# One core: attention and two MLPs, with the first 320 queries' probabilities kept in fp32 and turned by TensorE

## The chip, the cores and the metric

One core of a Trainium2 chip runs the program. The metric is device microseconds (us) of one execution; lower is better. The time of a kernel is the median of its runs. Engines: PE is TensorE's matmul side, PEld its weight load, DVE VectorE, ACT ScalarE, POOL GpSimd, SP the sync engine that issues DMAs.

## The reference

q, k and v are fp32, the MLPs' weights 64-bit floats. For most products the kernel splits a value into a high and a low fp16 half. Batch 4, 8 heads, 576 positions, head size 64; model width 512, inner width 2048.

```python
q_rot, k_rot = rotate(q), rotate(k)
scores = q_rot @ k_rot^T / sqrt(D)
scores = scores - max(scores, axis=-1)
attn = exp(scores)
attn = attn / (sum(attn, axis=-1) + 1e-9)
x = (attn @ v), heads side by side            # 2304 x 512
h = x @ moe_w_in;   x = (h * sigmoid(1.702 h)) @ moe_w_out
h = x @ moe2_w_in;  x = where(h > 0, h, exp(h) - 1) @ moe2_w_out
```

## The kernel before

**Tiling.** The 2304 queries are cut into nine blocks: batch 0 into three (128, 192 and 256 queries, the numbers 0, 1 and 2), every other batch into two (320 and 256). The 8 heads are worked on in pairs, hp 0 to 3. A unit (`s_units`) is one chunk of 128 queries of one head pair, or the last 64 queries of both heads laid on the two halves of the partitions (the tail). For each unit PE makes the fp32 scores (L689), DVE takes the negative row maximum (L694), ACT the exponentials with their sums (L698, tile E), DVE the reciprocal (L705, L709). Then the probabilities are scaled and split: the fp16 high half by ACT or DVE (`hi`, L714 or L716), the fp16 remainder by DVE (`lo`, L720), both in one tile Ehl. A transposing DMA on SP (L729, for a tail L726) writes them turned, keys on the partitions, into the tile et.

**Product with V.** `av_unit` multiplies et with V, which has been scaled and split into fp16 halves as well (`v_prep`, L652 and L655, with three small DMAs L659 to L661 that shift copies by half a tile): 14 products per head, the two heads on the two column halves of the array (L757). ACT and DVE write the result as two fp16 halves x (L760, L764).

**MLPs.** `first_mlp` multiplies x of the four head pairs with W1i (L808, 12 matmuls per unit of 128 inner columns), ACT and DVE form the activation (L811, L814, L823, L826, into ghl), and L845 multiplies with W1o; the results go to DRAM (y_d). The second MLP reads them back (L1040 to L1167).

**Weights.** `Weight` loads 64-bit pieces of 128 x 512 (L418; W1i's into ghl, which is empty then, W1o's into its own end), makes fp32 of them (ACT L425 and L432, DVE L439 and L444), takes a bound of their norms by PE (L462: sums against ones, gathered in one PSUM bank per weight that is held from the first sum to the last), brings the maximum over partitions (L346, L350, L353), and then scales and splits in place (ACT L499 or DVE L501, and DVE L505).

**What sets the order.** The program is a plan: `op` notes an operation with the engines that can run it and a cost on each, the operations that it follows, a key and the buffers that it needs. `Plan.run` goes through an own clock, gives every free engine the ready operation of the smallest key whose buffers are free, and emits the instructions in that order. TUNE holds numbers that are added to keys or costs, BUFS how many buffers there are: two score tiles of two banks each, one bank for products with V, and three banks "m" for everything else on PE (turns of q and k, L808, L845, sums). So engines work through fixed lists of instructions, and another number in TUNE is another list on every engine.

**The beginning.** `prep` loads k and q of one head pair on SP (four DMAs, L563 and L564), DVE applies the rotation with a table `tab` (L568, L572, L576), PE turns the result (L581, with the identity `eye`), ACT copies it out of PSUM (L586). `start` loads `eye` and `tab` on SP (L544, L545).

## Time and profile before

| | |
|---|---|
| runs | 1043.17, 1038.73, 1040.77 us; median 1040.77 |
| profiled execution | 1040.95 us, span in the trace 1039.2 us |
| PE busy | 959.6 us (92%), 7754 instructions |
| DVE busy | 864.1 us (83%), 1695 instructions |
| ACT busy | 603.8 us (58%), 1161 instructions |
| mean granted clock of PE | 0.954 of 2.4 GHz |
| DMA | 109.44 MB in 224062 packets, 372 issues |

The profile's times begin with the span. A group of rows gives for each line, engine and shape the count, the busy time, the mean of one, and the idle time ahead of it with its releaser. A busy sum is a share of the whole span; what a stage is worth is read from the stretch in which it lies.

### The profile page before, as it was taken

Reading aid. Unit: us, or ns where it says so; the run is one execution under the profiler, and the core shown is the slowest. Engines: PE = TensorE matmul, PEld = TensorE weight load, DVE = VectorE, ACT = ScalarE, POOL = GpSimd, SP = SyncE. Lnnn points to the kernel's source line nnn. Section 1 sums busy time; section 2 is a strip of 40 time slices with the busy share of each in tenths; the row PEclk is TensorE's granted clock in tenths of the full one; section 3 lists DMA queues with packets and bytes.
Section 4 is the critical chain, followed back from the end, with each engine's and each line's share of the span. In section 5 each row is a group of like instructions: output and inputs, shape, how many; then the busy total and the mean of one; then the engine's idle time right before and its main releaser. Section 6 shows DMA issues by size and latency. Waiting matters only on the chain. (4 is left out here: it accounts for less than half of the span.)

```text
span 1039.2 us, 19888 instructions
## 1 busy us (share of the span) xinstructions
PE 959.6 (92%) x7754; PEld 682.4 (66%) x7754; DVE 864.1 (83%) x1695; ACT 603.8 (58%) x1161; POOL 0.4 (0%) x6
## 2 busy tenths in 40 slices
PE   2447899999999999999999999999989999999997
PEld 2225588877766677766688778644436845855886
DVE  6999999887999689888765969899999579579474
ACT  4788797675687577666453739575355145145142
POOL 0000000000000000000000000000000000000000
PEclk8555899999999999999999999999999999999999
DMA  8899757896678856755635433610000100100100
GB/s 261 299 232 203 136 82 133 153 184 114 135 132 183 126 104 123 134 92 109 110 71 164 161 108 108 216 43 1 29 13 21 51 11 18 50 16 5 42 16 21
DMA packets 224062, 109.44 MB, mean 105 GB/s; under 512 B 187872, under 2 KB 213088, under 8 KB 223968
## 3 DMA queue, kind: packets, MB, share of 16 engines
q1 hardware_dynamic: 223968, 108.17, 46.7%
q8 instruction: 61, 1.00, 0.4%
q14 instruction: 33, 0.27, 0.1%
HBM read 53.61 MB, written 9.44 MB: 61 GB/s over the span
## 5 line engine op out<-in xcount | busy, mean ns | idle before, releaser
L808 PE MATMUL m<-x,wi 128*128 128x256 f16 (+3 forms) x1728 | 199.9, 275 | 2.1 <-DVE wi L505 1.7
L845 PE MATMUL m<-ghl,wo 128*128 128x256 f16 (+3 forms) x1728 | 198.2, 273 | 0.2 <-DVE wo L505 0.2
L1040 PE MATMUL m<-yhl,w2i 128*128 128x512 f16 (+1 forms) x960 | 190.2, 360 | 4.7 <-DVE e L1051 4.5
L808 PEld LDWEIGHTS <-wi 128*128 128x128 f16 x1728 | 157.6, 99 | 45.7 <-issue 14.7
L845 PEld LDWEIGHTS <-wo 128*128 128x128 f16 x1728 | 155.7, 98 | 41.7 <-issue 12.5
L1040 PEld LDWEIGHTS <-w2i 128*128 128x128 f16 x960 | 94.4, 98 | 98.5 <-issue 7.8
L698 ACT ACTIVATE E<-s,st 128x576 f32<-128x576 f32 x144 | 106.0, 737 | 67.8 <-DVE st L694 60.8
L720 DVE SCALAR_TENSOR_TENSOR Ehl<-E,st,Ehl 128x576 f16<-128x576 f32 x144 | 114.8, 810 | 9.9 <-ACT Ehl L714 9.5
L694 DVE TENSOR_REDUCE st<-s 128x1 f32<-128x576 f32 x144 | 106.4, 749 | 7.9 <-PE s L689 7.8
L689 PE MATMUL s<-qkT 64*128 64x288 f32 (+1 forms) x640 | 108.2, 459 | 4.1 <-ACT E L698 4.0
L714 ACT ACTIVATE Ehl<-E,st 128x576 f16<-128x576 f32 x105 | 79.9, 772 | 31.3 <-DMA et<-Ehl 10.1
L1043 ACT ACTIVATE e<-m,y_c 128x512 f32<-128x512 f32 (+1 forms) x80 | 50.7, 637 | 73.2 <-issue 48.7
L689 PEld LDWEIGHTS s<-qkT 64*128 64x128 f32 (+1 forms) x640 | 56.4, 189 | 33.1 <-issue 10.6
L1116 PEld LDWEIGHTS <-g 128*128 128x128 f16 x714 | 69.5, 98 | 8.7 <-issue 0.7
L811 ACT ACTIVATE t<-m,hsc 128x320 f32<-128x320 f32 (+3 forms) x96 | 55.3, 576 | 18.6 <-PE m L808 17.4
L1136 DVE SCALAR_TENSOR_TENSOR x<-z,eo,x 128x256 f32<-128x256 f32 x49 | 23.4, 482 | 48.9 <-PE z L1116 48.6
L823 ACT ACTIVATE ghl<-t 128x320 f16<-128x320 f32 (+3 forms) x96 | 49.7, 520 | 19.5 <-DVE t L814 19.2
L757 PE MATMUL av<-et,v 128*64 128x256 f16 (+3 forms) x720 | 52.8, 291 | 6.6 <-DMA et<-Ehl 5.9
L814 DVE SCALAR_TENSOR_TENSOR t<-t,m 128x320 f32<-128x320 f32 (+3 forms) x96 | 52.5, 547 | 7.6 <-ACT t L811 6.9
L826 DVE SCALAR_TENSOR_TENSOR ghl<-t,ghl 128x320 f16<-128x320 f32 (+3 forms) x96 | 52.6, 550 | 6.1 <-ACT ghl L823 5.9
L1116 PE MATMUL z<-wo,g 128*128 128x256 f16 x504 | 56.3, 273 | 0.0
L1051 DVE SCALAR_TENSOR_TENSOR e<-m,y_c,e 128x512 f32<-128x512 f32 (+1 forms) x80 | 55.0, 690 | 0.4
(160 smaller groups left out, 1233.1 us busy)
## 6 DMA issues: line engine op xcount, KB each, us to landing
R<-in_moe_w_out_dram SPq DMA_DIRECT2D x18, 512.0 KB, 3.7
ghl<-in_moe_w_in_dram SPq DMA_DIRECT2D x16, 512.0 KB, 6.1
R<-in_moe_w_in_dram SPq DMA_DIRECT2D x16, 512.0 KB, 4.2
wo<-in_moe_w_out_dram SPq DMA_DIRECT2D x14, 512.0 KB, 5.8
R<-in_k_dram SPq DMA_DIRECT2D x16, 256.0 KB, 3.0
R<-in_q_dram SPq DMA_DIRECT2D x16, 256.0 KB, 3.4
V<-in_v_dram SPq DMA_DIRECT2D x4, 1024.0 KB, 6.9
R<-y_d SPq DMA_DIRECT2D x8, 512.0 KB, 4.0
```

The costliest lines, as they stand in the source:

```text
L689: nc.tensor.matmul(o, X[r, t:t + (TAIL if h is None else P)], X[r, NS * w:NS * w + NS], start=True, stop=True)
L694: nc.vector.tensor_reduce(out=st["t"][:, a:a + 1], in_=take(hS[a])[:, :, 0:NS], axis=AX.XY, op=ALU.max, negate=True)
L698: nc.scalar.activation(out=take(hE[a]).rearrange("p (c f) -> p c f", c=2), in_=take(hS[a])[:, :, 0:NS], func=AF.Exp, bias=t[:, a:a + 1], s ...
L714: nc.scalar.activation(out=X16[:, 0:S], in_=take(hE[a]), func=AF.Copy, scale=r)
L720: nc.vector.scalar_tensor_tensor(out=X16[:, S:2 * S], in0=E, scalar=r, in1=X16[:, 0:S], op0=ALU.mult, op1=ALU.subtract)
L757: nc.tensor.matmul(ps[64 * a:64 * a + 64, 0:N], W[:, a, j, :] if w == 2 else V[:, w, a, j, :], T[:, a, blk, 0:N], start=i == 0, stop=i == ...
L808: nc.tensor.matmul(ps, W1i.lhs(kk, u, wl), x[:, xl, 0:N], start=kk == 0 and i == 0, stop=kk == KD - 1 and i == 2)
L811: nc.scalar.activation(out=flat(ht), in_=flat(hM), func=AF.Tanh, scale=hsc[b][:, 1:2])
L845: nc.tensor.matmul(ps[:, 0:N], W1o.lhs(f, d, wl), (gh, gl)[xl][:, f, g0:g0 + N], start=f == 0 and i == 0, stop=f == KF - 1 and i == 2)
L1040: nc.tensor.matmul(ps[:, 0:n], W2i.lhs(kk, u, wl), Y[:, xl, kk, 0:n], start=kk == 0 and i == 0, stop=kk == KD - 1 and i == 2)
L1051: nc.vector.scalar_tensor_tensor(out=t[:, 0:n], in0=take(hM)[:, 0:n], scalar=st["c"][:, 0:1], in1=t[:, 0:n], op0=ALU.mult, op1=ALU.max)
L1116: nc.tensor.matmul(ps, AT[A](p, gi, P * tt), BT[B](p, wl), start=p == 0 and i == 0, stop=p == 7 and i == 2)
```

## The change

Blocks 0 and 1 (the first 320 queries of batch 0, `WHOLE`) take another way from the exponentials to x. The probabilities stay fp32: one operation scales E in place (`norm`, by ACT or DVE), L761 or L763 of the changed kernel; there is no remainder and no Ehl. PE turns E against the identity, four blocks of 128 keys for each head and chunk (`turn`, L768), and the last 64 keys of both heads by a plain product (`turn_tail`, L774); ACT or DVE copies them from a bank "m" to et, read as fp32 (`put`, `put_tail`, L778 or L780). The product takes raw fp32 V: ten matmuls, the two heads on the column halves (`mm32`, L827 and L829), and V's scale enters when x is split. No transposing DMA is issued for these blocks. V of batch 0 is still split, since block 2 needs it. The loads of `tab` and `eye`, in the other sequence, and W1i's first two pieces are issued by ACT's queue. TUNE has other numbers everywhere and two new ones, so every engine's list is new; from the second half of PE's list to its end the lists are the same instructions in the same order.

```diff
 TUNE = dict(
...
+    w2i2=-436.9305624813725, w2o2=-980.4720244049131, pt=438.78214921243733, pv=136.99546015091275,
...
+    WHOLE = (0, 1)
...
-                    nc.sync.dma_start(out=flat(c).bitcast(I32), in_=s)
+                    ENG[e].dma_start(out=flat(c).bitcast(I32), in_=s)
...
-                ld = op(*dma_in(P * 4096), load, after, kc, need=[(stage(c), h)])
+                cost = dma_in(P * 4096)
+                if tag == "w1i" and i < 2:
+                    cost = {"act": 500}, cost[1]
+                ld = op(*cost, load, after, -1e6 if tag == "w1i" and i < 2 else kc, need=[(stage(c), h)])
...
     def start(e):
-        nc.sync.dma_start(out=eye, in_=tab_d[:, 18:20, :].rearrange("p a d -> p (a d)"))
-        nc.sync.dma_start(out=tab, in_=tab_d[:, 0:18, :])
+        ENG[e].dma_start(out=tab, in_=tab_d[:, 0:18, :])
+        ENG[e].dma_start(out=eye, in_=tab_d[:, 18:20, :].rearrange("p a d -> p (a d)"))
...
-    begin = op({"dma": 480}, 1600.0, start, key=TUNE["tab"])
+    begin = op({"act": 1000}, 3200.0, start, key=-2e6)
...
-            nc.vector.tensor_scalar(out=t, in0=t, scalar1=1e-9, scalar2=DOWN, op0=ALU.add, op1=ALU.mult)
+            nc.vector.tensor_scalar(out=t, in0=t, scalar1=1e-9, scalar2=1.0 if n in WHOLE else DOWN, op0=ALU.add, op1=ALU.mult)
...
+        if n in WHOLE:
+            hP = [("tp", i, x) for x in range(2 if h is None else 3)]
...
+            def norm(e, a):
+                r, E = st["t"][:, 4 + a:5 + a], take(hE[a])
+                if e == "act":
+                    nc.scalar.activation(out=E, in_=E, func=AF.Copy, scale=r)
+                else:
+                    nc.vector.tensor_scalar(out=E, in0=E, scalar1=r, scalar2=None, op0=ALU.mult)
+
+            def turn(e, a):
+                ps = take(hP[a])
+                for c in range(4):
+                    nc.tensor.transpose(ps[:, P * c:P * c + P], take(hE[a])[:, P * c:P * c + P], eye)
+
+            def turn_tail(e):
+                ps = take(hP[-1])
+                for a in range(2):
+                    x = a if h is not None else 0
+                    nc.tensor.matmul(ps[64 * a:64 * a + 64, 0:m], take(hE[x])[:, 512:S], eye if h is not None else eye[:, 64 * a:64 * a + 64], start=True, stop=True)
...
+            od = []
+            for a in heads:
+                od.append(op({"act": c_act(S, ptr=1), "dve": c_dve(S, 2, ptr=1)}, lambda e, a=a: norm(e, a), [o5], key + a, use=[hE[a]], port=True))
+                ot = op({"pe": 4 * 107 + 100.0}, lambda e, a=a: turn(e, a), od[-1:], key + a - TUNE["pt"], need=[("m", hP[a])], use=[hE[a]])
+                trs.append(op({"act": c_act(512, True) + (50 if h is None else 0), "dve": c_dve(512) + (60 if h is None else 0)}, lambda e, a=a: put(e, a), [ot], key + a - TUNE["pv"], use=[hP[a], hT]))
+            ot = op({"pe": 2 * 280.0}, turn_tail, od, key + 1 - TUNE["pt"], need=[("m", hP[-1])], use=hE)
+            trs.append(op({"act": c_act(m, True), "dve": c_dve(m)}, put_tail, [ot], key + 1 - TUNE["pv"], use=[hP[-1], hT]))
+            return
...
+        def mm32(e):
+            T, ps = take(hT).rearrange("p a s f -> p (a s f)").bitcast(F32), take(hA)
+            for c in range(5):
+                for a in range(2):
+                    r = slice(64 * a, 64 * a + 64)
+                    V = take(("vs", b))[:, 2 * hp + a, c, :]
+                    if c < 4:
+                        k = (4 * a + c) * N
+                        nc.tensor.matmul(ps[r, 0:N], V, T[:, k:k + N], start=c == 0, stop=False)
+                    else:
+                        nc.tensor.matmul(ps[r, 0:N], V[r], T[r, 8 * N:9 * N], start=False, stop=True)
...
-            nc.scalar.activation(out=take(hx)[:, 0, 0:N], in_=take(hA)[:, 0:N], func=AF.Copy, scale=DOWN)
+            nc.scalar.activation(out=take(hx)[:, 0, 0:N], in_=take(hA)[:, 0:N], func=AF.Copy, scale=vsc[b]["s"] if w else DOWN)
```

How the lists move is shown at three places. In the rows a name's number tells one tile or buffer from another.

The first is the beginning of the queues that issue DMAs. SP before (R is the tile of k and q of a head pair, ghl takes W1i's raw pieces):

```order
L563 DMA R_85<-in_k_dram 128x2x256
L564 DMA R_85<-in_k_dram 64x2x64
L563 DMA R_85<-in_q_dram 128x2x256
L564 DMA R_85<-in_q_dram 64x2x64
L544 DMA eye<-in_rope_dram 128x128
L545 DMA tab<-in_rope_dram 128x1152
L418 DMA ghl<-in_moe_w_in_dram 128x1024 x2
```

and in the changed kernel SP, and after it ACT:

```order
L567 DMA R_87<-in_k_dram 128x2x256
L568 DMA R_87<-in_k_dram 64x2x64
L567 DMA R_87<-in_q_dram 128x2x256
L568 DMA R_87<-in_q_dram 64x2x64
L419 DMA ghl<-in_moe_w_in_dram 128x1024 x2
```

```order
L548 DMA tab<-in_rope_dram 128x1152
L549 DMA eye<-in_rope_dram 128x128
L419 DMA ghl<-in_moe_w_in_dram 128x1024 x2
L426 ACT_TABLE_LOAD
L426 ACTIVATE wi<-ghl 128x512 x2
```

The table has gone from the sixth place of SP's list to the first of ACT's, and SP's own first four are the same.

The second is DVE at block 0's last head pair. Before (E_661 and E_665 are its two heads' exponentials, Ehl_706 and Ehl_716 their halves):

```order
L705 TENSOR_SCALAR st<-st 128x2
L709 RECIPROCAL st<-st 128x2
L716 TENSOR_SCALAR Ehl_706<-E_661,st 128x576
L716 TENSOR_SCALAR Ehl_716<-E_665,st 128x576
L764 SCALAR_TENSOR_TENSOR x_714<-av_669,x_714 128x128
L505 SCALAR_TENSOR_TENSOR wi<-wi,w1i_s 128x512
L694 TENSOR_REDUCE st<-s_708 128x1
L720 SCALAR_TENSOR_TENSOR Ehl_706<-E_661,st,Ehl_706 128x576
L694 TENSOR_REDUCE st<-s_710 128x1
L505 SCALAR_TENSOR_TENSOR wi<-wi,w1i_s 128x512
L720 SCALAR_TENSOR_TENSOR Ehl_716<-E_665,st,Ehl_716 128x576
```

and in the changed kernel (E_608 and E_646 are that pair; ACT scales the other head's):

```order
L713 TENSOR_SCALAR st<-st 128x2
L717 RECIPROCAL st<-st 128x2
L763 TENSOR_SCALAR E_608<-E_608,st 128x576
L509 SCALAR_TENSOR_TENSOR wi<-wi,w1i_s 128x512
L428 TENSOR_SCALAR wo<-wo 128x512
L838 SCALAR_TENSOR_TENSOR x_673<-av_649,v_s,x_673 128x128
L505 TENSOR_SCALAR wi<-wi,w1i_s 128x512
L440 SCALAR_TENSOR_TENSOR wo<-wo 128x512
L702 TENSOR_REDUCE st<-s_667 128x1
```

The two remainders L720 are gone, and DVE goes from one scaling to W1i's remainders (L509) and W1o's conversion (L428, L440) and on to the next maxima.

The third is PE after a product of block 1 (av_966 before is its first head pair, s_1008 the scores of its third). Before:

```order
L757 LDWEIGHTS vsh_380
L757 MATMUL av_966<-et_803,vsh_380 64x192
L346 MATMUL m_1005<-eye,v_a 1x128
L689 MATMUL s_1008<-qkT_238 128x288
L689 MATMUL s_1010<-qkT_238 128x288
```

and in the changed kernel the work between a unit of L885 and the product of block 1's first head pair (E_702, E_726 and E_730 its exponentials, m the banks, et_790 the turned ones):

```order
L885 MATMUL m_753<-x_738,wi 128x128
L768 MATMUL m_794<-eye,E_726 128x128 x4
L774 MATMUL m_803<-eye,E_702 64x128
L774 MATMUL m_803<-eye,E_726 64x128
L768 MATMUL m_808<-eye,E_730 128x128 x4
L774 MATMUL m_817<-eye,E_730 64x64 x2
L697 MATMUL s_824<-qkT_202 64x288 x4
L827 MATMUL av_833<-et_790,V_112 64x192 x8
L829 MATMUL av_833<-et_790,V_112 64x192 x2
```

Turns of four blocks and small products against the identity (two of the pair's three turns are in these rows) stand in PE's list where before transposing DMAs stood in SP's, and each has a bank "m" of its own.

## Rows read from the trace of the kernel before

**Rows 1.** Busy time in stretches: us, then PE, PEld, DVE, ACT, POOL busy, PEclk, DMA share, GB/s
```profile
8.30:62.50 54.20, 20.16 (x140) 14.65 (x140) 50.65 (x79) 40.13 (x77) 0.00 (x0) 0.61 0.90 291
62.50:95.50 33.00, 19.62 (x178) 12.68 (x178) 30.63 (x66) 24.29 (x48) 0.00 (x0) 0.50 0.97 216
95.50:131.50 36.00, 29.97 (x320) 21.96 (x320) 34.14 (x80) 28.45 (x64) 0.00 (x0) 0.81 0.77 143
0.00:95.50 95.50, 39.79 (x318) 27.34 (x318) 81.27 (x144) 65.71 (x124) 0.44 (x6) 0.61 0.90 256
137.82:1039.20 901.38, 883.55 (x7049) 627.61 (x7046) 743.09 (x1456) 504.79 (x965) 0.00 (x0) 1.00 0.41 88
```

**Rows 2.** Timeline of PE from the first L808 to 174 us: start, us, what
```profile
97.62 3.40 PE L808 MATMUL m<-x,wi 128*128 128x128 f16 x48
...
105.08 1.02 PE L757 MATMUL av<-et,v 128*64 128x192 f16 x20
105.93 0.50 PE L757 MATMUL av<-et,vsh 128*64 128x192 f16 x8
106.36 0.38 PE L346 MATMUL m<-eye,v_a 128*1 128x128 f32 x2
...
107.84 1.51 PE L808 MATMUL m<-x,wi 128*128 128x128 f16 x24
...
131.47 0.23 PE L808 MATMUL m<-x,wi 128*128 128x128 f16 x1 [1.68 <-DVE wi L505]
...
137.82 0.83 PE L845 MATMUL m<-ghl,wo 128*128 128x128 f16 x12
...
140.57 1.24 PE L689 MATMUL s<-qkT 64*128 64x288 f32 x8
...
171.25 0.55 PE L581 MATMUL m<-eye,T 128*128 128x128 f32 x3
...
172.90 0.88 PE L581 MATMUL m<-eye,T 128*128 128x128 f32 x6
```

**Rows 3.** Waits of PE, 138 to 620 us: us in total, times, longest
```profile
PE av L757 <- DMA et<-Ehl: 1.8, 4, 0.7
...
PE m L581 <- ACT qkT L586: 0.8, 1, 0.8
```

**Rows 4.** Waits of DVE before the mark, and of PE from 62 us to it
```profile
DVE T L568 <- DMA tab<-in_rope_dram: 8.4, 1, 8.4
...
PE av L757 <- DMA et<-Ehl: 4.0, 5, 2.0
```

**Rows 5.** The SP queue at the start, and issues: KB each, median us to landing
```profile
0.73 0.46 SPq L563 DMA_DIRECT2D R<-in_k_dram  x1
...
2.68 0.62 SPq L564 DMA_DIRECT2D R<-in_q_dram  x1
...
3.98 0.43 SPq L545 DMA_DIRECT2D tab<-in_rope_dram  x1
...
tab<-in_rope_dram SPq DMA_DIRECT2D x1, 576.0 KB, 4.3
R<-in_k_dram SPq DMA_DIRECT2D x16, 32.0 KB, 3.1
```

**Rows 6.** Groups by shape: count, busy us, mean ns, idle before
```profile
L720 DVE SCALAR_TENSOR_TENSOR Ehl<-E,st,Ehl 128x576 f16<-128x576 f32 x144 | 114.8, 810 | 9.9 <-ACT Ehl L714 9.5
...
L586 ACT ACTIVATE qkT<-m 128x384 f32<-128x384 f32 x48 | 22.1, 489 | 10.0 <-PE m L581 9.4
...
L505 DVE SCALAR_TENSOR_TENSOR wi<-wi,w1i_s 128x512 f16<-128x512 f32 x16 | 11.8, 741 | 0.0
```

**Rows 7.** Timeline of PE at the lower clock: one turn group and one score group
```profile
38.24 0.87 PE L581 MATMUL m<-eye,T 128*128 128x128 f32 x3 [0.64 <-DVE T L576]
...
77.57 2.29 PE L689 MATMUL s<-qkT 64*128 64x288 f32 x8
```

More of the change, by code (lines that the diff above doesn't have):

```diff
@@ L580, in turn @@
             for s in range(3):
-                nc.tensor.transpose(ps[:, P * s:P * s + P], take(hT)[:, 3 * g + s].rearrange("p h d -> p (h d)"), eye)
+                t = take(hT)[:, 3 * g + s].rearrange("p h d -> p (h d)")
+                nc.tensor.transpose(ps[:, P * s:P * s + P], t, eye)
         def put(e, g):
@@ L610 @@
     v_scaled = {}
+    v_loaded = {}
     def v_view(b, hp):
@@ L623, in ld_ @@
                 nc.sync.dma_start(out=t[64 * a:64 * a + 64, :, 4, :], in_=v[b, :, 512:S, :].rearrange("h p d -> p h d"))
-        ld = op(*dma_in(1311e3, 3), ld_, [], ka, need=[("V", h)])
+        ld = v_loaded[b] = op(*dma_in(1311e3, 3), ld_, [], ka, need=[("V", h)])
         for hp in range(NP):
@@ L644, in v_prep @@
         for hp in range(NP):
+            if all(n in WHOLE for n in range(NB) if blocks[n][0] == b):
+                break
             ks = last_u[fb[b], hp] - TUNE["vs"]
@@ L740, in s_units, with whole, out_, put @@
         cost = dma_tr(2 * S) if h is not None else ({"dma": 2600}, 1700.0)
+        if n in WHOLE:
+            hP = [("tp", i, x) for x in range(2 if h is None else 3)]
+            m = TAIL if h is None else P
+            o = N - TAIL if h is None else chunks.index(j) * P
+            def whole():
+                T = take(hT).rearrange("p a s f -> p (a s f)").bitcast(F32)
+                return T[:, 0:8 * N].rearrange("p (a c f) -> p a c f", a=2, c=4), T[:, 8 * N:9 * N]
+            def norm(e, a):
[13 more added lines that the diff above has]
+                    nc.tensor.matmul(ps[64 * a:64 * a + 64, 0:m], take(hE[x])[:, 512:S], eye if h is not None else eye[:, 64 * a:64 * a + 64], start=True, stop=True)
+            def out_(e, dst, src):
+                if e == "act":
+                    nc.scalar.activation(out=dst, in_=src, func=AF.Copy)
+                else:
+                    nc.vector.tensor_copy(dst, src)
+            def put(e, a):
+                T, ps = whole()[0], take(hP[a])
+                if h is None:
+                    for a in range(2):
+                        out_(e, T[:, a, :, o:o + m], ps.rearrange("p (c a f) -> p a c f", c=4, a=2)[:, a])
+                else:
+                    out_(e, T[:, a, :, o:o + m], ps.rearrange("p (c f) -> p c f", c=4))
+            def put_tail(e):
+                out_(e, whole()[1][:, o:o + m], take(hP[-1])[:, 0:m])
+            od = []
[6 more added lines that the diff above has]
+            return
@@ L757, in mm @@
                     nc.tensor.matmul(ps[64 * a:64 * a + 64, 0:N], W[:, a, j, :] if w == 2 else V[:, w, a, j, :], T[:, a, blk, 0:N], start=i == 0, stop=i == len(slots) - 1)
+        def mm32(e):
+            T, ps = take(hT).rearrange("p a s f -> p (a s f)").bitcast(F32), take(hA)
+            for c in range(5):
+                for a in range(2):
+                    r = slice(64 * a, 64 * a + 64)
[3 more added lines that the diff above has]
+                        nc.tensor.matmul(ps[r, 0:N], V, T[:, k:k + N], start=c == 0, stop=False)
+                    else:
+                        nc.tensor.matmul(ps[r, 0:N], V[r], T[r, 8 * N:9 * N], start=False, stop=True)
+        w = n in WHOLE
         def hi(e):
-            nc.scalar.activation(out=take(hx)[:, 0, 0:N], in_=take(hA)[:, 0:N], func=AF.Copy, scale=DOWN)
+            nc.scalar.activation(out=take(hx)[:, 0, 0:N], in_=take(hA)[:, 0:N], func=AF.Copy, scale=vsc[b]["s"] if w else DOWN)
         def lo(e):
             x = take(hx)
-            nc.vector.scalar_tensor_tensor(out=x[:, 1, 0:N], in0=take(hA)[:, 0:N], scalar=DOWN, in1=x[:, 0, 0:N], op0=ALU.mult, op1=ALU.subtract)
+            nc.vector.scalar_tensor_tensor(out=x[:, 1, 0:N], in0=take(hA)[:, 0:N], scalar=vsc[b]["s"] if w else DOWN, in1=x[:, 0, 0:N], op0=ALU.mult, op1=ALU.subtract)
         key = float(last_u[n, hp]) - TUNE["av"]
-        o = op({"pe": 14 * (N / 2.4 + 4) + 180}, mm, trs + [v_ready[b, hp]], key, need=[("av", hA)], use=[hT, hV, hW])
-        o = op({"act": c_act(N, True)}, hi, [o], -1e4, need=[("x", hx)], use=[hA])
+        if w:
+            o = op({"pe": 5 * 4 * (N / 2.4 + 4) + 300}, mm32, trs + [v_loaded[b]], key, need=[("av", hA)], use=[hT, ("vs", b)])
+        else:
+            o = op({"pe": 14 * (N / 2.4 + 4) + 180}, mm, trs + [v_ready[b, hp]], key, need=[("av", hA)], use=[hT, hV, hW])
+        o = op({"act": c_act(N, True, 1 if w else 0)}, hi, [o, v_scaled[b] if w else None], -1e4, need=[("x", hx)], use=[hA])
         x_ready[n, hp] = op({"dve": c_dve(N)}, lo, [o], -1e4, use=[hA, hx])
```

11 lines of the change are left out of this document (5 added, 6 removed).

## Prediction

> **What bounds the kernel now.** I read the stretches first [rows 1]. In 137.82:1039.20 TensorE (PE) is busy 883.55 of 901.38 us at the full clock: from there on the kernel is PE's work, and a us that PE starts later is a us at the end. Ahead of it PE idles: 20 busy us of the 54 from 8.3 to 62.5, and 19.62 of the next 33, at a granted clock of 0.50, the lower level, 1.2 GHz. VectorE (DVE) is busy 50.65 of 54.2, 30.63 of 33 and 34.14 of 36: it sets the pace of the start. ScalarE (ACT) has over a fifth of its time left. The transfers' share is 0.90 and 0.97 up to 95.5.
>
> The mark that I reckon with is the first product of the second weight of the first MLP, line L845, at 137.82 [rows 2]. By the order of both kernels PE has done the same ahead of it (16 units of L808, four products of probabilities and V for each of blocks 0 and 1, the scores of both blocks and of one head pair and two chunks of block 2), so all that the change adds lies before the mark. Two things differ: the turns of a fifth head pair (three groups, 0.55 and 0.88 us at 171 to 174 [rows 2]) stand ahead of it now, and one pair of small products for a maximum over partitions (L346 at 0.38 and its partner, 0.8 together) behind it. In the second half of PE's order nothing is moved. So: new time = old time + shift of the mark - 1.4 + 0.8. In the stretch between, PE's waits are small, 5.4 us from 138 to 620, the longest of which and one on a copy by ACT I show [rows 3].
>
> **The start.** DVE's first instruction waits 8.4 us, for the table [rows 4], the sixth transfer of the sync queue (SP), issued at 3.98 and landed 4.3 us later [rows 5]. ACT now issues it first, by the same row's landing at 0.73 + 4.3 = 5.0; k and q stay on SP, the last at 2.68 + 3.1 = 5.8. Nothing was there to share with ACT's four issues before, so the bounds are a gain of 0 and of 8.36 - 5.8 = 2.6; I take 2.0, near the upper, because the bytes wanted (some 1.2 MB) are 4 us at the 291 GB/s of [rows 1]. The Trainium skill, DMA: Bandwidth & Descriptors, section "Issuing engines are not separate DMA queues", speaks against it: such DMAs share the same engines, and only the time to initiate them is saved. By that rule alone the gain would be nearly 0 and the sum 2 us higher; the row shows that the initiating, six in a row, is itself 3.25 us here.
>
> **DVE up to the first L808.** It waits for the fourth x of block 0 (DVE, L764). Ahead of that the order has, now against before: 0 instead of 11 remainders L720 (11 x 0.810 = 8.9 [rows 6]), 4 instead of 11 of the W1i remainders L505 (7 x 0.741 = 5.2; the rest comes later, under PE), and small items of both signs, -1.2 net. Durations summed: 94.0 before, 78.7 now. Summed durations overlap (94.0 stand for 81.27 busy us up to 95.5 [rows 1]), so 15.3 are 13.2 us. With the 2.0: L808 from 97.6 [rows 2] to 82.4. That is the bound by DVE. PE has a say too: between the scores of head pair 3 and that point the order gives PE three full scores and one tail (2.3 each), four turns of four blocks (4/3 of 0.87), two tail turns, two fp32 products and some sums, about 22 us at the lower clock [rows 7], in a stretch of about 18. Up to 88, then. I take 84, nearer DVE's bound, since at the full clock these 22 would be 12. Covered by this: the W1o pieces that SP now issues ahead of the last W1i piece, ten instead of five (2.6 MB, 9 us at the rate of [rows 1]), which delay W1i's last conversions by some 4 us of DVE; their room is the stretch that the remainders leave. If DVE weren't relieved, those 4 us would be paid.
>
> **ACT.** Up to the eighth tanh the order gives it 126.5 us of summed durations against 116.8: copies of turned probabilities out of PSUM, which have no row before (nearest: L586, 384 columns, 0.489 [rows 6]; for 512 columns about 0.6, an estimate from it). That makes its busy share before the mark some 82% instead of 72%. It costs nothing while ACT keeps room; where it is gone, see the second rival.
>
> **PE from the first L808 to the mark.** Before: 192 L808 at 24 in 1.51 (12.1), seven scores at 1.24 (8.6), four products at 1.35 (5.4; L757 at 105.08 and 105.93 overlap), small ones 2.7: 28.8 us of work in 40.2 elapsed [rows 2]. So 11.4 went to waits and to a clock at 0.81 in the mean [rows 1]. Added: 12 turns of four 128-blocks, at 0.88 for six 0.59 each (7.1); 8 tail turns, plain fp32 products with 128 columns against the identity, nearest row L346 (0.38), 0.4 each (3.2); four fp32 products for 192 queries. These have no row. Nearest: fp32 scores, 4 x 288 columns in pairs in 1.24 us. Ten products of 192 are 1920 columns, so 1920/1152 x 1.24 = 2.07 if the two heads run side by side as they do there, 4.1 if not; before 1.35. I take 2.07 (+2.9 for four). With the fifth pair's turns (+1.4) and without the small products (-0.8): 28.8 + 13.8 = 42.6 us. For waits and clock I take 5 instead of 11.4, about half: the five waits for transposing DMAs go (4.0 us up to the mark [rows 4]) and PE has turns to put into the gaps; 0 and 11.4 stay as ends. Mark: 84 + 42.6 + 5 = 131.6.
>
> The transposing DMAs of both blocks (L729, L726) leave SP's queue; weights and next loads behind them go out earlier, and nobody waits for those.
>
> **The sum.** Mark -6.2 (137.8 to 131.6), behind it -0.6: -6.8. The profiled execution took 1040.95 (span 1039.2 and 1.75 around it), 0.2 above the median of 1040.77. 1040.95 - 6.8 = **1034.2**. About 0.5%, 5.2 us, is what a measurement of this kernel can tell from no change; the forecast lies just beyond it.
>
> **Rivals.**
> *DVE's bound is reached.* PE never waits and gets the full clock early. Then the last W1i slice decides, for which PE waits at 131.47 [rows 2]: 131.8 us of summed DVE work stand before it now, 122.1 after, 8.4 us at the same ratio, plus the 2.0: mark at 127.4, time 1029.9. For it: DVE is the busy one today. Against: PE's 42.6. Chance 0.14.
> *The handing over of PSUM banks.* Turns, sums and L808 share three "m" banks, and one is held by W1o's sums most of the time. Block 1 alone turns through 20 banks, each PE, then an ACT copy, then free. At 2.4 us each these equal my 47.6; at 2.8 the mark is at 140 and the time 1042. For it: PE waited for such a copy already (L581 for ACT's L586 [rows 3]). Against: a bank's round is a turn of 0.6 and a copy of 0.6, and 2.4 is twice that. Chance 0.12.
> *The clock stays low.* It was 0.50 in the whole stretch 62.5:95.5, in which PE was busy 19.62 of 33 [rows 1]. If turns and waits keep it there, L808 begins at 88 and the waits with the low clock cost 8.4: mark 139, time 1041.6. Chance 0.15. The Trainium skill, TensorE: Matmul & The Clock Gate, Part 4 "PE-mode transpose", says that transposes don't count as busy for the clock; by that rule this rival gains; the rows don't contradict it, since the lower clock held through every L581 before 96.
> *Slower: the two heads' fp32 products don't share the array.* Each then costs 4.1 instead of 2.07 in block 1 (4 x 2.07 = 8.3), and at the lower clock 2.5 more for the two of block 0 that end last (5.0): mark 144.9, time 1047.5. It decides if the product of a block with 192 queries takes over 3.4 us, at which nothing is left of the gain. For it: no row shows fp32 on column halves. Against: fp16 there (L757) and fp32 on row halves (L689) both overlap. Chance 0.15.
> That the early loads don't do what they say is 2 us: 1036, inside the rivals without change.
>
> **How the numbers follow.** Forecast (1030.5 to 1035.5) 0.44 and DVE's bound 0.14: faster 0.58. Banks and clock: same 0.27. Slower 0.15. The range runs from 1024 (DVE's bound, and the 5.4 us of small waits between 138 and 620 gone) to 1046 (most of the bank and clock cases and the beginning of the slower one); what is left out is the larger half of that one and a little below.
>
> **What would show it.** Right: DVE begins at 6 to 6.5; no L720 before the mark; the first product of W1i at 82 to 86 and of W1o at 130 to 133; fp32 products of 192 queries at 2.0 to 2.3 us; PE's busy sum about 20 us higher; behind the mark the same 901 us less 0.6. Wrong: a clock of 0.50 far beyond 97, ACT copies as the releaser of most of PE's waits, or a stretch behind the mark that is longer by over 3 us, which my sum holds to be unmoved.

## The result and the profile after

| | before | changed |
|---|---|---|
| median of the runs | 1040.95 us (6 runs, 1038.73 to 1044.23) | 1031.6 us (6 runs, 1029.66 to 1035.1) |
| profiled execution, its span | 1040.95, 1039.2 | 1031.25, 1029.5 |
| first L808 / L885 in the span | 97.62 | 82.63 |
| the mark, first L845 / L922 | 137.82 | 125.59 |

The ratio is 0.9909, 95% interval [0.9892, 0.9926]: 0.9% less time, and the interval lies wholly below 1. The profiled execution is 9.7 us shorter, where the prediction's sum had -6.8. The stretches of the changed kernel, first the one that answers to the first of [rows 1], then up to the first product of W1i, from there to the mark, and the rest:

```profile
core 0: us, PE busy (x) PEld busy (x) DVE busy (x) ACT busy (x) POOL busy (x), PEclk, DMA share, GB/s
8.30:62.50 54.20, 30.93 (x208) 23.28 (x208) 50.19 (x81) 45.37 (x89) 0.00 (x0) 0.63 0.91 307
62.50:82.63 20.13, 16.25 (x136) 10.43 (x133) 19.56 (x48) 17.92 (x39) 0.00 (x0) 0.82 0.38 105
82.63:125.59 42.96, 39.44 (x438) 29.04 (x438) 42.74 (x98) 40.58 (x93) 0.00 (x0) 1.00 0.33 93
125.59:1029.50 903.91, 884.36 (x7045) 627.37 (x7041) 740.97 (x1465) 504.91 (x966) 0.00 (x0) 1.00 0.42 87
```

The same view of the kernel before, for its own stretch from the first L808 to the mark:

```profile
97.62:137.82 40.20, 34.17 (x386) 26.38 (x385) 37.64 (x93) 31.25 (x69) 0.00 (x0) 0.82 0.72 131
```

The stretch is 2.8 us longer than before but begins 15.0 us earlier. All three engines are nearly full in it: DVE 42.74, ACT 40.58 and PE 39.44 of 42.96 us. Up to 62.5 PE is busy 30.93 us, where it was 20.16. The transfers' share falls from 0.97 [rows 1] to 0.38 behind 62.5; no probability goes through a transposing DMA there any more.

What the new path costs on PE, by shape, in that stretch (the first row is the products with W1i), and then the products with W1i and those of block 1 with V in the kernel before (97.62 to 137.82). Columns: count, busy us, mean ns, idle before:

```profile
L885 PE MATMUL m<-x,wi 128*128 128x128 f16 x192 | 12.7, 219 | 0.0
L768 PE MATMUL m<-eye,E 128*128 128x128 f32 x48 | 7.5, 283 | 1.3 <-ACT et L778 1.2
L827 PE MATMUL av<-et,V 128*64 128x192 f32 x64 | 6.1, 332 | 0.0
L829 PE MATMUL av<-et,V 64*64 64x192 f32 x16 | 2.2, 348 | 0.0
L774 PE MATMUL m<-eye,E 128*64 128x128 f32 x16 | 1.8, 298 | 1.0 <-DVE t L891 0.5 <-ACT et L778 0.5
L774 PE MATMUL m<-eye,E 128*64 128x64 f32 x16 | 1.3, 246 | 0.1
```

```profile
L808 PE MATMUL m<-x,wi 128*128 128x128 f16 x192 | 14.3, 240 | 1.7 <-DVE wi L505 1.7
L757 PE MATMUL av<-et,v 128*64 128x192 f16 x80 | 5.8, 302 | 0.7 <-DMA et<-Ehl 0.7
L757 PE MATMUL av<-et,vsh 128*64 128x192 f16 x32 | 2.8, 307 | 0.0
```

Four fp32 products take 6.1 + 2.2 = 8.3 us, 2.07 each. The four fp16 ones that they replace took 5.8 + 2.8 = 8.6 us, part of it at the lower clock, with 28 matmuls in each instead of ten (the rows have 20, since the profile lists each plain fp32 matmul twice). The turns are what is added: 7.5 + 1.8 + 1.3 = 10.6 us. In the kernel before the granted clock was half again at about 116 to 119, 123 to 130 and 133 to 136 us; in the changed one it is full from 70 us to the mark, and the 192 products with W1i take 12.7 us where they took 14.3.

The start, by the longest of DVE's waits up to 128 us, and from ACT's queue the issues of the table and of W1i's first two pieces (start, us, engine):

```profile
DVE T L572 <- DMA R<-in_q_dram: 9.2, 1, 9.2
```

```profile
0.73 0.42 ACTq L548 DMA_DIRECT2D tab<-in_rope_dram  x1
1.66 3.86 ACTq L419 DMA_DIRECT2D ghl<-in_moe_w_in_dram  x2
```

DVE begins 0.8 us later than before (8.4 [rows 4]), and for q, no longer for the table.

Behind the mark, the last L808 was at 642.3 and the last L885 is at 629.4, 12.9 earlier. From there to the end the lists are the same, yet the profiled execution is 3.2 us longer there (396.9 before, 400.1 now). 2.5 of it is one group, here first in the changed kernel, then in the one before:

```profile
1010.32 10.48 PE L1193 MATMUL z<-wo,g 128*128 128x256 f16 x72
```

```profile
1022.50 8.02 PE L1116 MATMUL z<-wo,g 128*128 128x256 f16 x72
```

The granted clock was 0.50 from about 1008.5 to 1015.3 in the profiled execution of the changed kernel, after PE had waited 3 us, and stayed at full in that of the kernel before after the same stall. The list doesn't decide it: over the fourteen profiles of this case the group takes 8.02 us in five and 9.7 to 10.8 us in nine. Two of the nine have the lists of the kernel before (10.65 and 10.71), three of the five those of the changed one.

### The profile page after: what moved, and what is told of

Same layout as the page of the kernel before. It is cut to its first block, busy times and chain, and to the rows that moved or that the text cites. A ratio compares the mean times of both kernels' runs of the same rounds, so it can differ in the third digit from the quotient of the medians.

```text
span 1029.5 us, 19948 instructions
## 1 busy us (share of the span) xinstructions
PE 971.0 (94%) x7818; PEld 690.1 (67%) x7818; DVE 853.4 (83%) x1688; ACT 610.1 (59%) x1184; POOL 0.4 (0%) x6
## 5 line engine op out<-in xcount | busy, mean ns | idle before, releaser
L885 PE MATMUL m<-x,wi 128*128 128x256 f16 (+3 forms) x1728 | 198.8, 273 | 1.2 <-DVE t L891 1.1
L922 PE MATMUL m<-ghl,wo 128*128 128x256 f16 (+3 forms) x1728 | 199.0, 273 | 0.0
L885 PEld LDWEIGHTS <-wi 128*128 128x128 f16 x1728 | 156.0, 98 | 43.0 <-issue 13.6
L922 PEld LDWEIGHTS <-wo 128*128 128x128 f16 x1728 | 155.5, 98 | 42.3 <-issue 13.4
L697 PE MATMUL s<-qkT 64*128 64x288 f32 (+1 forms) x640 | 104.1, 440 | 2.8 <-ACT E L706 2.8
L728 DVE SCALAR_TENSOR_TENSOR Ehl<-E,st,Ehl 128x576 f16<-128x576 f32 x124 | 99.2, 810 | 4.6 <-ACT Ehl L722 3.5
L722 ACT ACTIVATE Ehl<-E,st 128x576 f16<-128x576 f32 x86 | 65.2, 772 | 26.2 <-DMA et<-Ehl 8.8
L888 ACT ACTIVATE t<-m,hsc 128x320 f32<-128x320 f32 (+3 forms) x96 | 55.6, 579 | 14.5 <-PE m L885 14.1
L1193 PE MATMUL z<-wo,g 128*128 128x256 f16 x504 | 58.8, 279 | 0.0
L1193 PEld LDWEIGHTS <-ghl 128*128 128x128 f16 x420 | 41.0, 98 | 9.0 <-ACT ghl L1092 2.4
```

The lines of the kernel that those rows point to most:

```text
L697: nc.tensor.matmul(o, X[r, t:t + (TAIL if h is None else P)], X[r, NS * w:NS * w + NS], start=True, stop=True)
L722: nc.scalar.activation(out=X16[:, 0:S], in_=take(hE[a]), func=AF.Copy, scale=r)
L728: nc.vector.scalar_tensor_tensor(out=X16[:, S:2 * S], in0=E, scalar=r, in1=X16[:, 0:S], op0=ALU.mult, op1=ALU.subtract)
L885: nc.tensor.matmul(ps, W1i.lhs(kk, u, wl), x[:, xl, 0:N], start=kk == 0 and i == 0, stop=kk == KD - 1 and i == 2)
L888: nc.scalar.activation(out=flat(ht), in_=flat(hM), func=AF.Tanh, scale=hsc[b][:, 1:2])
L922: nc.tensor.matmul(ps[:, 0:N], W1o.lhs(f, d, wl), (gh, gl)[xl][:, f, g0:g0 + N], start=f == 0 and i == 0, stop=f == KF - 1 and i == 2)
```

## The experiments

Every run is compared with runs of the kernel before on the same chip (1040.98, 1042.61, 1041.61 and 1041.22 us in the four groups of runs). The changed kernel's own ratio above is the other measure.

**What is VectorE worth?** My theory was that DVE sets the pace of the start and that taking the remainders off it lets the rest move up. The first run puts idle work back into the changed kernel (the lists else as they are):

```diff
                     nc.vector.tensor_scalar(out=E, in0=E, scalar1=r, scalar2=None, op0=ALU.mult)
+                for _ in range(2):
+                    nc.vector.scalar_tensor_tensor(out=spare, in0=tab[:, 0:9, :].rearrange("p s d -> p (s d)")[:, 0:NS], scalar=1.0, in1=spare, op0=ALU.mult, op1=ALU.subtract)
```

> The changed kernel with VectorE's removed work put back as idle work: at each of the 20 scalings of blocks 0 and 1 VectorE does two instructions on constants of 288 columns (some 0.43 us each), on which nobody waits. Theory (VectorE sets the start, and its 42.74 busy us of the 42.96 from the first L885 to the mark bind there too): the first L885 at 88 to 90 instead of 82.6, the mark (first product of the second weight) at 137 to 142 instead of 125.6, time 1043 to 1048. Rival (PE with its turns, or ACT with its copies, binds from the first L885 on): first L885 later by 6, but the mark by under 8, time 1037 or less.

Measured: 1050.86 us, ratio 1.0095 [1.0079, 1.0110]. The 40 instructions are 0.457 us each, 18.3 in all, and cost 19.3 us against the changed kernel's 1031.6, more than the theory had. The first L885 product came at 88.9, the mark at 145.3 us. Added work on DVE is paid in full.

The second run takes the remainders off the kernel before. In blocks 0 and 1 the low halves are zeros (left out: the low half of these probabilities); all else, the transposing DMAs too, stays:

```diff
+            if n in (0, 1):
+                nc.vector.memset(X16[:, S:2 * S], 0.0)
+                return
             nc.vector.scalar_tensor_tensor(out=X16[:, S:2 * S], in0=E, scalar=r, in1=X16[:, 0:S], op0=ALU.mult, op1=ALU.subtract)
```

> The kernel before, its lists as they are, with the low half of the probabilities of blocks 0 and 1 left out: VectorE sets it to zero (about 0.25 us) where it worked out the remainder (0.81). The transposing DMAs stay. Theory (it is VectorE's remainders that held the start): the first L808 at 91 to 93 instead of 97.6, the mark at 127 to 131 instead of 137.8, time 1031 to 1035. Rival (the transposing DMAs and the low clock held it): first L808 at 96 or later, mark at 135 or later, time 1038 or more.

Measured: 1039.35 us (10 runs, 1035.19 to 1042.36), ratio 0.9983 [0.9969, 0.9997]. The rival's time, and my theory fell here. The groups up to the mark, in the kernel before and in this one, show that the work was really gone, 10.0 us of it:

```profile
L720 DVE SCALAR_TENSOR_TENSOR Ehl<-E,st,Ehl 128x576 f16<-128x576 f32 x20 | 16.0, 806 | 0.0
```

```profile
L721 DVE MEMSET Ehl<- 128x288 uint32 x20 | 6.0, 298 | 0.2
```

Yet the first expert product came at 97.4 instead of 97.6 and the mark at 137.3 instead of 137.8. DVE's waits from 60 to 140 us, before and with the short rest, tell where the time went (us in total, times, longest):

```profile
DVE st L694 <- PE s L689: 3.2, 7, 1.0
DVE x L764 <- ACT x L760: 0.6, 1, 0.6
DVE t L814 <- ACT t L811: 0.5, 1, 0.5
```

```profile
DVE st L694 <- PE s L689: 6.0, 7, 1.3
DVE x L767 <- ACT x L763: 3.4, 6, 0.8
DVE t L817 <- ACT t L814: 0.7, 2, 0.4
DVE wo L505 <- ACT wo L499: 0.6, 1, 0.6
DVE wi L505 <- ACT wi L499: 0.4, 1, 0.4
DVE R L439 <- ACT wo L425: 0.4, 1, 0.4
DVE wo L439 <- ACT wo L432: 0.3, 1, 0.3
```

DVE now waits 11.8 us where it had waited 4.3: for scores that stand behind the products on PE, and for the outputs of those products. The 7.5 us are three quarters of what was taken off. (This profiled execution, at 1042.36 us, was the slowest of the ten.) PE's rows tell what the products stood for. Here block 0's first and third product, in the kernel before and then with the short rest:

```profile
66.19 1.22 PE L757 MATMUL av<-et,v 128*64 128x128 f16 x19 [0.40 <-DMA et<-Ehl]
83.06 1.23 PE L757 MATMUL av<-et,v 128*64 128x128 f16 x19 [0.67 <-DMA et<-Ehl]
```

```profile
66.04 1.23 PE L760 MATMUL av<-et,v 128*64 128x128 f16 x19 [0.94 <-DMA et<-Ehl]
83.33 1.23 PE L760 MATMUL av<-et,v 128*64 128x128 f16 x19 [0.61 <-DMA et<-Ehl]
```

DVE had written the last low half of these two pairs 1.6 and 1.4 us earlier, but SP began to issue the transposing DMAs only 0.2 and 1.0 us earlier, and the product came 0.15 us earlier and 0.3 later. So the trip through SP's queue and the transposing DMA took up what DVE gave. DVE was busy almost throughout in the kernel before, and it still wasn't what held the stretch alone.

The third run adds the idle instructions of the first to the kernel before, behind L720:

```diff
+            for _ in range(2 if n in (0, 1) else 0):
+                nc.vector.scalar_tensor_tensor(out=spare, in0=tab[:, 0:9, :].rearrange("p s d -> p (s d)")[:, 0:NS], scalar=1.0, in1=spare, op0=ALU.mult, op1=ALU.subtract)
```

> The kernel before with the same 40 idle VectorE instructions of 0.457 us (18.3 us) that cost the changed kernel 19 us, two behind each of the 20 remainder halves of the first two blocks. Taking 10 us off VectorE there had given nothing. If the stretch of the kernel before is held by the trip through the transposing DMA, with VectorE waiting beside it, at most half of it shows: under 1051. If VectorE holds it too and the lists are merely fitted to the lengths that the instructions had, it shows in full: 1057 to 1062.

Measured: 1054.77 us, ratio 1.0126 [1.0106, 1.0147]: 13.5 us for 18.2 us (40 of 0.454), between the two expectations. So in the kernel before a us more on DVE costs 0.74, and a us less gives about 0.16 (1.6 for 10.0).

**The numbers and the path.** The change brings new numbers in TUNE, which write the lists anew, and a new path. Three runs take them apart. The new numbers with the old path:

```diff
-    WHOLE = (0, 1)
+    WHOLE = ()
```

> The changed kernel's numbers and its first loads by ScalarE, but no block treated in the new way: halves, remainders and transposing DMAs for all of batch 0, as before. If the order that the numbers set is what gained, 1031 to 1035 us. If the work taken off VectorE or the path by TensorE is what gained, the numbers alone give nothing: 1039 to 1046, the first L885 product no earlier than about 96 us, where the kernel before has it at 97.6 and the changed one at 82.6.

Measured: 1080.35 us, ratio 1.0367 [1.0346, 1.0388], 37.7 us slower than the kernel before and outside both expectations. The same with the low halves of blocks 0 and 1 filled with zeros, as above:

> The run above, with the remainder halves of the first two blocks filled with zeros by VectorE (left out: the low half of these probabilities) instead of computed: 20 x about 0.5 us less on VectorE, the transposing DMAs and products as before. The same edit on the kernel before took 10 us of work off VectorE and moved the first expert product by only 0.2 us, since VectorE then idled for scores and outputs. If that was only because the lists of the kernel before are fitted to VectorE's work, new numbers let it show: 1031 to 1036. If the trip through the transposing DMA holds the stretch whatever VectorE has to do, within 2 us of the run above.

Measured: 1075.97 us, ratio 1.0326 [1.0301, 1.0350]. That is 4.4 us below the run above, outside both expectations: here, too, the 10 us of DVE give less than half of themselves back. PE's waits up to 200 us, in the first of these two and in the changed kernel:

```profile
PE m L466 <- DVE ghl L440: 23.2, 8, 11.4
PE m L466 <- DVE wo L440: 17.4, 11, 3.8
PE s L697 <- ACT E L706: 13.6, 10, 2.1
```

```profile
PE m L466 <- DVE ghl L440: 15.4, 6, 11.6
PE m L586 <- DVE T L580: 11.2, 4, 3.8
PE s L697 <- ACT E L706: 2.8, 4, 1.4
...
PE m L466 <- DVE wo L440: 1.4, 3, 0.6
```

The waits for W1o's converted pieces are 17.4 us instead of 1.4: PE stands in front of sums and scores whose inputs the other engines have later in their lists. The order that the new numbers write is only good with the new path in it.

The third takes the numbers of before, with the two new ones (pt, pv) kept, and the new path:

```diff
 TUNE = dict(
-    tab=14.943572507220972, f_dve=7503.721787689248, f_act=378.3487104989394, f_pool=6747.827774550082, w1i2=416.7173416679817,
...
+    tab=-755.3495038560459, f_dve=3717.3294571158176, f_act=658.9801078794787, f_pool=2518.1827925442094, w1i2=409.947966353374,
...
+    pt=438.78214921243733, pv=136.99546015091275,
 )
```

> The new path for the first two blocks and the first loads by ScalarE, with the numbers of the kernel before (the two that exist only in the changed kernel kept). If the path is what gains, 1030 to 1036 and the first L885 product at 82 to 88 us. If the numbers are needed to place the turns, 1037 to 1046.

Measured: 1047.72 us, ratio 1.0052 [1.0032, 1.0072]. With the old numbers the new path (and the new first loads) makes the kernel 5.1 us slower, a little above the second expectation. DVE's rows up to 82.6 us, for W1i's remainders and the outputs, here and in the changed kernel:

```profile
L510 DVE SCALAR_TENSOR_TENSOR wi<-wi,w1i_s 128x512 f16<-128x512 f32 x8 | 5.9, 743 | 0.4 <-ACT wi L504 0.4
L839 DVE SCALAR_TENSOR_TENSOR x<-av,v_s,x 128x128 f16<-128x128 f32 (+1 forms) x3 | 1.1, 366 | 0.8 <-ACT x L835 0.8
```

```profile
L509 DVE SCALAR_TENSOR_TENSOR wi<-wi,w1i_s 128x512 f16<-128x512 f32 x4 | 3.0, 745 | 0.0
L838 DVE SCALAR_TENSOR_TENSOR x<-av,v_s,x 128x128 f16<-128x128 f32 x4 | 1.4, 346 | 0.0
```

DVE was as busy by then (69.1 us here, 69.8 there). With the old numbers it spent that time on W1i's remainders, and PE's first expert product stood at 99.6 us instead of 82.6: by then PE had done 56 of the turned pieces of L768's kind and 80 fp32 matmuls of the product, where the changed kernel's list has its first W1i product behind 32 and 64. Block 1's first product, at 75.5 us, stood ahead of block 0's third and fourth (84.4 and 92.2), and the first expert product needs the fourth; in the changed kernel all four of block 0 (43.6, 60.9, 72.3 and 79.4) come before block 1's first at 88.95. So neither part gains by itself: +37.7 and +5.1 us, and -9.4 together.

**The clock.** In the profiled execution of the kernel before the granted clock is half from 20 to 98 us, in that of the changed one from 22 to 70 (one-us windows; the times in the expectation are some 2 us early). To give PE more to do there, the score products of blocks 0 and 1 are issued twice:

```diff
-                    nc.tensor.matmul(o, X[r, t:t + (TAIL if h is None else P)], X[r, NS * w:NS * w + NS], start=True, stop=True)
+                    for _ in range(2 if n in (0, 1) else 1):
+                        nc.tensor.matmul(o, X[r, t:t + (TAIL if h is None else P)], X[r, NS * w:NS * w + NS], start=True, stop=True)
```

> The kernel before with the score products of its first two blocks issued twice, which leaves the result as it is and gives TensorE some 20 x 1.2 us of work more at full clock (twice that at half). In the kernel before the granted clock is half from 18.3 to 96.8 us, in the changed one full from 67.9. If the half clock in that stretch is what costs the kernel before its time and TensorE's idling is what keeps it low, the clock rises earlier and the time falls to 1034 to 1038. If the clock there costs little, the extra products lie on the chain and the time is 1041 to 1052.

Measured: 1047.35 us, ratio 1.0052 [1.0032, 1.0072]. The clock came up a few times in between (half at 21 to 36, 42 to 70, 72 to 80 and 89 to 100 us), the first expert product was at 100.4, and the time is the second expectation's. By itself this doesn't tell what the clock is worth, since the added products lie on the chain. The 53 runs of the kernel before in the four groups tell more. By the mean granted clock they fall into two lots: 27 at 0.947 to 0.960, as the profiled execution has it (0.954), with a median of 1042.1 us, and 26 at 0.975 to 0.992, with a median of 1040.9. Each lot is spread over 6 to 7 us, so the half clock of the start costs the kernel before about 1 us, if anything.

**The first loads.** W1i's first two pieces by SP, with table and identity left to ACT:

```diff
-                    ENG[e].dma_start(out=flat(c).bitcast(I32), in_=s)
+                    nc.sync.dma_start(out=flat(c).bitcast(I32), in_=s)
```

> The changed kernel, W1i's first two pieces issued by SP in its list's place (behind k and q of the first head pair), table and identity by ACT as before; every list of PE and DVE is the same. Theory (the 1 MB of W1i that ACT issues at 1.66 shares the DMA engines with q, so that q lands late and VectorE starts at 9.18 and not at 6.3): VectorE starts at 6.0 to 7.0, the first L885 at 80 to 81 (82.6 in the changed kernel), the time is 1 to 3 us below the changed kernel's 1031.6. Rival (the early weights are worth as much as q): VectorE starts earlier but waits for converted weights, first L885 within 1 us of 82.6, time within 1 us of 1031.6.

Measured: 1030.98 us, ratio 0.9907 [0.9892, 0.9922]. DVE began at 7.04 instead of 9.18, so W1i's 1 MB beside k and q is what made q late. The first L885 came at 81.9, the mark at 127.3 in the profiled execution: a head start of 2.1 us that is 0.7 at the first product and can't be told from nothing at the end, the rival's case. The second puts all first loads on SP:

```diff
-        ENG[e].dma_start(out=tab, in_=tab_d[:, 0:18, :])
-        ENG[e].dma_start(out=eye, in_=tab_d[:, 18:20, :].rearrange("p a d -> p (a d)"))
+        nc.sync.dma_start(out=tab, in_=tab_d[:, 0:18, :])
+        nc.sync.dma_start(out=eye, in_=tab_d[:, 18:20, :].rearrange("p a d -> p (a d)"))
```

> The changed kernel, all four loads that ACT issues put on SP: table and identity first, then k and q, then W1i. Theory (what counts is which bytes go first, not which queue issues them): k and q are issued 1 us later, VectorE starts at 7 to 8, the time is within 1.5 us of the run with only the weights on SP. Rival (ACT's queue is what helps): VectorE starts at 9 or later, the time is 2 us or more above that run.

Measured: 1033.69 us, ratio 0.9922 [0.9904, 0.9940]: not to be told from the changed kernel either, though 2.7 us above the run before it, as the rival had it. DVE began at 7.45, as the theory had it, so the issuing queue is worth 0.4 us of the beginning (7.04 with ACT's). Then it had to wait 1.9 us more for W1i's first piece at 10.1, and the first L885 came at 84.0. Its profile has something else, the granted clock. First this kernel's rows, then the changed kernel's:

```profile
20.00:40.00 20.00, 9.97 (x57) 7.49 (x58) 16.96 (x31) 17.48 (x36) 0.00 (x0) 1.00 0.91 307
40.00:58.00 18.00, 11.63 (x88) 8.11 (x86) 17.29 (x29) 16.73 (x34) 0.00 (x0) 1.00 0.92 344
```

```profile
20.00:40.00 20.00, 11.33 (x63) 8.19 (x63) 18.24 (x33) 19.05 (x38) 0.00 (x0) 0.55 0.92 321
40.00:58.00 18.00, 11.05 (x80) 8.05 (x80) 17.00 (x29) 16.37 (x33) 0.00 (x0) 0.50 0.91 323
```

With the same list PE had the full clock there in one execution and half of it in the other, and the first L885 came no earlier for it.

**What binds the changed kernel now?** Three runs, one per engine. DVE less: the maximum over half of the scores in blocks 0 and 1.

```diff
-in_=take(hS[a])[:, :, 0:NS], axis=AX.XY
+in_=take(hS[a])[:, 0:1, 0:NS] if n in WHOLE else take(hS[a])[:, :, 0:NS], axis=AX.XY
```

> The changed kernel, with VectorE's maximum for the first two blocks taken over half of the scores (the first 288 of 576 keys; any shift of the exponent cancels in the division), so that 20 instructions of 0.75 us take about 0.4; every list as it was. VectorE has some 7 us less to do. If VectorE binds the new kernel up to the first W1o product, as its 99.5% busy there says, and as the run with work put back gave about 1.05 us for each us, the time falls by 5 to 7 us: 1024.5 to 1027. If what is left is held by the order or by TensorE, 1029.5 to 1032.5.

Measured: 1030.54 us, ratio 0.9895 [0.9878, 0.9913]. The 20 maxima took 0.451 us each, 6.0 us less in all. The time is 1.1 us below the changed kernel's, 1.5 by the ratios, which its runs can't tell from nothing: the second expectation. ACT less, without the scaling of the probabilities:

```diff
-                if e == "act":
-                    nc.scalar.activation(out=E, in_=E, func=AF.Copy, scale=r)
-                else:
-                    nc.vector.tensor_scalar(out=E, in0=E, scalar1=r, scalar2=None, op0=ALU.mult)
+                pass
```

> The changed kernel without the division of the probabilities in the first two blocks (left out: the 20 scalings in place, 19 of them ScalarE's at 0.76 us), so ScalarE has 14.5 us less to do up to 113 us and the trip from the exponent to the turn is one instruction shorter. If VectorE alone binds, 1029 to 1033. If ScalarE or the length of the trip counts as well, 1020 to 1028.

Measured: 1030.59 us, ratio 0.9895 [0.9876, 0.9914]: 14.5 us less on ACT, nothing gained that can be told: the first expectation. PE more:

```diff
-                for c in range(4):
-                    nc.tensor.transpose(ps[:, P * c:P * c + P], take(hE[a])[:, P * c:P * c + P], eye)
+                for _ in range(2):
+                    for c in range(4):
+                        nc.tensor.transpose(ps[:, P * c:P * c + P], take(hE[a])[:, P * c:P * c + P], eye)
```

> The changed kernel with each turn of four columns' pieces issued twice (20 x 0.6 us, at half clock about twice that: some 12 to 17 us more for TensorE; the result is the same). TensorE's idle time is 33 us up to 68 us and 6.6 from there to 140. If VectorE alone binds, what TensorE adds is covered up to its slack: 1032 to 1037. If TensorE binds as much as VectorE behind 68 us, where 16 of the 20 lie, 1038 to 1046.

Measured: 1036.25 us, ratio 0.9949 [0.9930, 0.9967], 4.6 us above the changed kernel for 12 us (20 x 0.6) of PE work: the first expectation, in which PE's slack covers the larger part. The stretch 82.63:125.59 of the three profiles, in this order:

```profile
82.63:125.59 42.96, 39.55 (x440) 29.08 (x438) 40.57 (x97) 40.65 (x94) 0.00 (x0) 1.00 0.35 97
```

```profile
82.63:125.59 42.96, 38.43 (x420) 27.91 (x417) 41.98 (x98) 33.28 (x78) 0.00 (x0) 1.00 0.27 79
```

```profile
82.63:125.59 42.96, 41.84 (x438) 30.96 (x435) 41.13 (x98) 38.65 (x88) 0.00 (x0) 1.00 0.21 66
```

Relieve DVE (40.57 for 42.74) and ACT and PE are as full as they were; relieve ACT (33.28) and DVE is at 41.98; load PE (41.84) and the others begin to idle. Taking work off DVE alone or ACT alone no longer shortens the stretch; the three engines are within 3.5 us of each other. That the lists are fitted to the lengths that the instructions have is my reading of it; no run relieves two engines at once.

None of these versions is faster than the changed kernel by more than its runs scatter.

## Why the prediction was right in its number, and where it was wrong

- **The number: partly luck.** The mark came 6.0 us earlier than forecast (125.6 for 131.6), and the end lost 3.1 us against the forecast behind it (903.9 us for 901.4 - 0.6). Without the second miss the profiled execution would have been at about 1028, below the range of the main forecast.
- **PE bounds the kernel behind the mark, so a shift of the mark is a shift of the end: right.** In the eleven profiles that have the lists of one of the two kernels the mark lay between 124.0 and 151.9 us, and from it to the end it was 900.0 to 904.6 us. From the mark to the last L808 or L885 it was -0.7 us (12.9 - 12.2), as the -1.4 + 0.8 had it. Of the 3.2 us lost behind that, 2.5 are one group at a lower clock in that one execution. It is the case named as "longer by over 3 us", and since the same group is as long in runs with the lists of the kernel before, it is not a consequence of the change.
- **The start, -2.0: wrong.** The table was there at about 5.1 us (issued at 0.73 and landed 4.4 us later, by the view of the issues), but DVE then waited for q, until 9.18: +0.8 instead. The estimate that only k, q and table were on their way left W1i's pieces out, issued from 1.66 on; with these behind k and q on SP the first instruction came at 7.04. The Trainium skill, DMA: Bandwidth & Descriptors, section "Issuing engines are not separate DMA queues", says that DMAs issued by different engines run on the same DMA engines, so that issuing them side by side saves only the time of the issuing. The traces agree: which queue issues was worth 0.4 us (7.04 and 7.45), and W1i's pieces from a second queue put q off by 2.1.
- **DVE up to the first L885, -13.2 busy us and 84 us: right in the sum (83.39 busy us before, 69.75 now, -13.6; first product at 82.63), wrong as a cause.** I took DVE's busy share for the bound, so that less work there would be an earlier end. The short rest took 10.0 us off DVE and the product moved by 0.2. What moved it is the new order together with the new path. The transposing DMA is out of the trip from the exponentials to the product: for block 0's third and fourth pair that trip took 8.8 and 10.4 us before and takes 6.5 and 6.0 now, by the timelines, from the end of the second head's exponential to the first matmul. And the lists bring the fourth x before most of W1i's remainders. With the old numbers and about the same DVE work (69.1 us up to 82.6) the product stood at 99.6. That 82.63 is so near to DVE's bound of 82.4 is luck as well: the beginning was 2.8 us later than forecast, and DVE's idle time from its first instruction to the product fell from 5.9 to 3.7 us, which the sum didn't have. The busy times, of the kernel before and of the changed one:

```profile
0.00:97.62 97.62, 41.91 (x324) 28.42 (x325) 83.39 (x148) 67.79 (x129) 0.44 (x6) 0.60 0.90 256
0.00:82.63 82.63, 47.19 (x340) 33.71 (x341) 69.75 (x128) 64.57 (x128) 0.44 (x6) 0.71 0.77 252
```

- **PE's say, "up to 88": not needed.** The 22 us were reckoned at the lower clock, but the clock was full again from 70 us on, and PE was busy 16.25 of the last 20.13 us before the product.
- **PE to the mark, 42.6 + 5: over-sized.** It was 39.44 busy in 42.96. The terms hold one by one: fp32 products 8.3 (forecast 4 x 2.07), turns 7.5 (7.1), tail turns 1.8 + 1.3 (3.2), units of L885 12.7 (12.1), scores, by the same view, 5.5 + 3.6 (8.6). All lines of that view add up to 44.1 us, but PE was busy 39.44: groups of different lines overlap by 4.7 us where one follows the other at once, and I had added them end to end. Waits and clock were 3.5 instead of 5, the clock full throughout. So the stretch took 43.0 instead of 47.6 and began 1.4 earlier: mark at 125.6, 6.0 before the 131.6.
- **ACT, "costs nothing while it keeps room": right.** Up to the mark it is busy 84% (82% forecast), in the stretch from the first L885 94%, and taking 14.5 us off it gave nothing.
- **The rivals.** *DVE's bound reached* (mark 127.4, 1029.9) came nearest to the measured mark and time, but its reason holds by half: DVE is full (42.74 of 42.96) and added work on it is paid, but 6.0 us less on it gave about 1. *Banks*: PE waits for ACT's copies 1.2 + 1.1 us in 60:128, a fraction of the price. *Low clock*: wrong; from 70 us on it is full up to the mark, though 15 of the 20 turns of four lie behind that. The prediction's remark that the lower clock held through every L581 before 96 misreads the trace: the first nine, at 12.62 us, ran at a granted clock of 1.00, which fell at about 20 us. The Trainium skill, TensorE: Matmul & The Clock Gate, Part 4 "PE-mode transpose", says that transposes don't count as PE's being busy in the same way. No run here shows turns holding the clock down: with the turns doubled it was full from the start, and other work of PE lay between them. *Slower*: excluded by 2.07 us per product, where 3.4 had been the point that decides.
- **The signs.** The first product of W1i and the fp32 products came out as named. DVE's begin (9.18), the first product of W1o (125.6) and PE's busy sum did not: it is 11.4 us higher (971.0 for 959.6), not 20. Two remainders of block 2 (L728, from 123.1) lie before the mark, where none had been expected.

What stays open: which of the numbers matters, since they were only exchanged as a whole; and whether the kernel before, with its old path, could gain by an order of its own. That the time falls to 1031.6 only with path and numbers together is shown. That the trip through the transposing DMA was the other hold in the kernel before rests on the waits of DVE and PE in the short-rest run, not on a run that took that trip alone away.

## What to carry to other kernels

An engine that is busy 94% of a stretch may still not be what holds it: where lists are fixed in advance and fitted to the lengths, added work is paid (0.74 to 1.05 us per us here) and removed work is returned only in part (0.16 to 0.44 per us); in the kernel before three quarters of it turned into waits for the other engines. So don't price a removal by an engine's busy share alone; ask for each freed us what the next instruction in its list waits for. And a change of path and a change of order are one change: here each alone lost 5 and 38 us, and the two together gained 9.

## What the hardware showed that I had not expected

- The granted clock of the start isn't fixed by the list. The changed list had 0.50 to 0.55 from 20 to 58 us in one execution, another with the same PE list 1.00, and the run with doubled turns 1.00 throughout:

```profile
20.00:40.00 20.00, 13.01 (x77) 10.13 (x75) 19.21 (x34) 19.35 (x39) 0.00 (x0) 1.00 0.95 333
40.00:60.00 20.00, 13.14 (x93) 9.93 (x90) 18.31 (x30) 17.45 (x34) 0.00 (x0) 1.00 0.81 287
```

- It gained nothing there that can be told: these two had their first expert product at 84.0 and 85.0 us, the one at half clock at 82.6. Of the changed kernel's six runs the three with a mean granted clock of 0.995 or more took 1030.85, 1031.94 and 1032.91 us, the three with 0.982 or less 1029.66, 1031.25 and 1035.1.
- Ten fp32 products of 192 columns for two heads on two column halves take 2.07 us, no more than the 28 fp16 ones on split halves that they replace (8.3 and 8.6 us for four).
- The same stall of 3 us near the end was followed by half clock in one execution and by full clock in another, a difference of 2.5 us.
